# Moving the conversion of the first two weight tiles two pairs of heads ahead, in a fused attention and feed-forward kernel

## Chip, cores and metric

The kernel runs on one core of a Trainium2 chip. The metric is the device time of one execution in microseconds (us), as the median of several runs. TensorE is called PE here, VectorE DVE, ScalarE ACT, GpSimd POOL, and SP is the engine that issues the DMAs of this kernel. Each engine works through its own list of instructions in the order in which they stand.

## What is computed

Decay attention over 4 batches of 8 heads (576 positions, head size 64), then two feed-forward blocks on the 2304 x 512 result:

```python
scores = scale * np.matmul(q, k.transpose(0, 1, 3, 2))
decay = cum[:, :, :, None] - cum[:, :, None, :]        # cum: running sum of log f
scores = np.where(causal, -1e9, scores + decay)
attn = softmax(scores)                                  # max, exp, sum, divide
x = (attn @ v), heads side by side                      # 2304 x 512
h = np.maximum(x @ w_in, 0.0)                           # 512 -> 2048
x = h * h @ w_out                                       # 2048 -> 512
out = (sigmoid(x @ w_gate) * (x @ w_val)) @ w_out2      # 512 -> 1536 -> 512
```

Everything is wanted to float32 accuracy. The five weight matrices come in as float64.

## The kernel before

**Attention** works on 16 pairs of heads, p = 0 to 15. A pair goes through named steps, each a few instructions on one engine. S01, S2, S3 and S4 are the score matmuls on PE (L306, L379). R0a to R4 take the row minimum of the negated scores from PSUM on DVE (L284). X0a to X4 take the exponential on ACT (L292). N0, N2 and N3 form reciprocals of the row sums on DVE (L388, L389). M0a to M4 multiply by them on POOL (L394). G1 to G4 transpose on PE (L405, L411). E1 to E4 copy the transposed blocks into one SBUF tile, `pts`: E1 and E3 on ACT (L316), E2 and E4 on DVE (L318). PV multiplies by v on PE (L439, 14 matmuls in two passes each, so 28 in the trace: 8 that need E1 and E2, then 20 that need all of `pts`). xhi on ACT (L456) and xlo on DVE (L454) write the result into `xT`. All PSUM tiles of attention come from a ring of four, `pa0` to `pa3`, so a matmul can also wait for the step that read the tile's old contents.

The table ORDER (L471) is the pipeline. One iteration `it` runs every step of the table once, each for the pair `it - lag`, with the lag written behind the step. So in one iteration E3 and PV work on pair it - 2, while X4, X3, G and M work on it - 1 and S, R and X0 to X2 on `it`. The code of attention is under a manual schedule: its instructions stand on each engine as they are written. What comes after L497 is placed by a scheduler, which may put it among the last steps of attention too.

**Weights.** `w_load` (L103) loads one 512 KB tile of float64 words into a raw buffer, of which there are three. `w_conv` (L119) turns it into two float32 tiles, `hl`: an ACT step (L131), four DVE steps (L132, L133, L134, L137), an ACT step (L140) and a POOL step (L141), each waiting for the one before. L140 is issued on ACT right behind L131 when nothing is written between. `conv_load(n)` loads the first n tiles of the queue, `conv_some(1)` converts the next one. The first up-projection needs "in" tile 0 at its start and tile 1 some 12 us later.

The lines that place the first two tiles:

```python
if it == NP - 4:
    conv_load(2)
if it in (NP, NP + 1):
    conv_some(1)
```

NP is 16. Iterations 16 and 17 are the two in which no new pair starts: the pipeline drains there. A third tile, "out" tile 0, has a free raw buffer from the start and is loaded by the scheduler right behind the two.

**Feed-forward.** `up` (L516) does an up-projection block (L524) into a ring of eight PSUM banks, `down` (L565) a down-projection (L588). Between them the activations go to DRAM and back.

Of the kernel before, what the change touches and what calls it, by code (L numbers as in the profile page):

```python
# [40 lines left out]
def kernel(  # L41
# [17 lines left out]
    NP = BH // 2  # L59
# [85 lines left out]
    def conv_load(n):  # L145
        for key, m, _, _ in conv_q[:n]:
            if (key, m) not in wraw:
                w_load(key, m)

    def conv_some(n):  # L150
        for _ in range(min(n, len(conv_q))):
            w_conv(*conv_q.pop(0))
            conv_load(3)
# [334 lines left out]
    for it in range(min(lags), NP + max(lags)):  # L488
        for nm_, lag in steps:
            p = it - lag  # L490
            if 0 <= p < NP:
                STEP[nm_](p)
        if it == NP - 4:
            conv_load(2)
        if it in (NP, NP + 1):
            conv_some(1)
    order.__exit__(None, None, None)  # L497
    att.close()
# [152 lines left out]
```

## Time and profile before

| | us |
|---|---|
| median of 3 runs | 1052.91 (1052.67 to 1055.0) |
| the profiled execution | 1052.9 |
| its span, first to last instruction | 1051.2 |
| PE busy in the span | 1027.0 (98%) |
| attention, from the start to the first up-projection matmul | 209.3 |

The page's first part gives the busy time of each engine. The chain that ended last is followed back from the last instruction, at each step to what released it. The timeline gives each instruction with its start, its length, and in brackets the idle time of its engine in front of it with the engine, tile and line that ended it. The windows view cuts the span into stretches and gives for each the busy times and PEclk, the clock granted to PE (1.00 is 2.4 GHz, 0.50 is 1.2 GHz).

### The profile page before, as it was taken

What the parts mean: (1) busy time and instruction counts of PE and PEld (TensorE: products, weight loads), DVE (VectorE), ACT (ScalarE), POOL (GpSimd) and SP (SyncE); (2) the same over time, 40 slices, a digit from 0 to 9 for tenths busy, and PEclk for the clock granted to TensorE, in tenths of its full rate; (3) what the DMA queues carried; (4) which work ended last, traced back from release to release, by engine and by line L of the source; (5) the groups of instructions that cost most, each with busy time, mean ns of one, the idle gap of its engine ahead of it and who ended that gap; (6) DMA issues with size and microseconds to landing.
All of it is one profiled execution on the core that took longest, in us unless ns stands there. A gap on an engine that the chain in (4) does not pass through costs nothing.

```text
span 1051.2 us, 15632 instructions
## 1 busy us (share of the span) xinstructions
PE 1027.0 (98%) x5675; PEld 859.7 (82%) x5675; DVE 503.3 (48%) x1067; ACT 399.5 (38%) x854; POOL 220.7 (21%) x306
## 2 busy tenths in 40 slices
PE   4999999899999999999999999999999999999998
PEld 3788788588888888888888988888888888888887
DVE  2878778597666675233232414444444421232222
ACT  2888778544444343233232323222222211122222
POOL 3776666532122211000000002111111120000000
PEclk7999999899999999999999999999999999999999
DMA  5333333066765565333332214434433211244333
GB/s 121 71 86 87 70 83 106 21 187 199 210 211 188 188 204 167 101 93 98 101 93 83 85 51 119 132 124 132 132 119 107 94 46 46 78 138 140 99 123 110
DMA packets 125965, 121.98 MB, mean 116 GB/s; under 512 B 63552, under 2 KB 91200, under 8 KB 125888
## 3 DMA queue, kind: packets, MB, share of 16 engines
q1 hardware_dynamic: 125888, 120.99, 38.6%
q8 instruction: 44, 0.72, 0.3%
q14 instruction: 33, 0.27, 0.1%
HBM read 83.06 MB, written 37.90 MB: 115 GB/s over the span
## 4 chain that ended last, share of the span: by engine, by line
PE 95%; SPq 2%; DMA 1%; DVE 0%; issue 0%; ACT 0%; POOL 0%; POOLq 0%
PE ps L524 47%; PE ps L588 33%; PE pa L439 4%; PE pa L306 4%; PE pa L405 3%; PE pa L270 2%; PE pa L379 2%; SPq L196 1%; DMA cr<-cum_d 1%; PE pa L411 1%; SPq L200 1%; POOL pt L394 0%; ACT pt L292 0%; SPq L356 0%; ACT pts L316 0%
## 5 line engine op out<-in xcount | busy, mean ns | idle before, releaser
L524 PE MATMUL ps<-xT,hl 128*128 128x512 f32 (+1 forms) x2400 | 494.4, 368 | 0.0
L524 PEld LDWEIGHTS ps<-xT,hl 128*128 128x128 f32 x2400 | 418.4, 189 | 75.8
L141 POOL TENSOR_TENSOR hl<-wf,hl 128x512 fp32r<-128x512 f32 x68 | 93.1, 1377 | 565.1 <-ACT hl L140 548.6
L562 DVE TENSOR_TENSOR gg<-gi,gg 128x512 fp32r<-128x512 f32 (+1 forms) x140 | 90.5, 647 | 237.0 <-ACT gg L561 236.9
L588 PE MATMUL ps<-gg,hl 128*128 128x512 f32 (+1 forms) x960 | 197.3, 368 | 0.0
L588 PEld LDWEIGHTS ps<-gg,hl 128*128 128x128 f32 x960 | 167.2, 189 | 30.0
L561 ACT ACTIVATE gg<-gi 128x512 fp32r<-128x512 f32 (+1 forms) x140 | 82.4, 589 | 251.1 <-PE ps L588 227.8
L588 PE MATMUL ps<-hl,gg 128*128 128x512 f32 x648 | 147.1, 389 | 0.0
L588 PEld LDWEIGHTS ps<-hl,gg 128*128 128x128 f32 x648 | 121.6, 188 | 25.2
L394 POOL TENSOR_TENSOR pt<-pt,sm 128x128 f32<-128x128 f32 (+2 forms) x144 | 105.8, 767 | 53.8 <-DVE sm L389 53.8
L616 DVE TENSOR_TENSOR r<-ps,r 128x512 f32<-128x512 f32 (+1 forms) x60 | 38.2, 636 | 138.1 <-PE ps L524 133.3
L292 ACT ACTIVATE pt<-pt,nm 128x128 f32<-128x128 f32 (+1 forms) x144 | 82.5, 583 | 10.1 <-DVE nm L284 10.0
L137 DVE SCALAR_TENSOR_TENSOR wf<-wraw,wtmp 128x512 int32<-128x512 int32 x68 | 57.6, 848 | 57.4 <-POOL hl L141 56.0
L614 ACT ACTIVATE r<-ps 128x512 f32<-128x512 f32 (+1 forms) x60 | 32.9, 548 | 122.5 <-PE ps L524 122.5
L140 ACT ACTIVATE hl<-wf 128x512 fp32r<-128x512 f32 x68 | 42.9, 631 | 88.6 <-DVE wf L137 47.2
L131 ACT ACTIVATE wtmp<-wraw 128x512 f32<-128x512 f32 x68 | 45.2, 666 | 74.5 <-DMA wraw<-in_moe_w_in_dram 23.4
L284 DVE CUSTOM_DVE_ANT_0 pt<-pa,maskc 128x128 f32<-128x128 f32 (+2 forms) x144 | 67.0, 514 | 12.0 <-PE pa L306 11.4
L543 ACT ACTIVATE r<-ps 128x512 f32<-128x512 f32 (+1 forms) x80 | 42.5, 547 | 43.2 <-DMA g<-r 38.2
L544 DVE TENSOR_TENSOR r<-r 128x512 f32<-128x512 f32 (+1 forms) x80 | 50.7, 646 | 17.0 <-ACT r L543 17.0
L439 PE MATMUL pa<-pts,vn 128*64 128x320 f32 (+4 forms) x448 | 49.2, 371 | 3.9 <-ACT pts L316 3.9
L439 PEld LDWEIGHTS pa<-pts,vn 128*64 128x64 f32 x448 | 30.5, 141 | 22.9 <-ACT pts L316 4.4
L134 DVE SCALAR_TENSOR_TENSOR wtmp<-wraw,wtmp 128x512 int32<-128x512 int32 x68 | 48.0, 708 | 2.2
(79 smaller groups left out, 685.4 us busy)
## 6 DMA issues: line engine op xcount, KB each, us to landing
g<-r SPq DMA_DIRECT2D x112, 256.0 KB
gi<-g SPq DMA_DIRECT2D x112, 256.0 KB
wraw<-in_moe_w_out_dram SPq DMA_DIRECT2D x28, 512.0 KB
wraw<-in_moe_w_in_dram SPq DMA_DIRECT2D x16, 512.0 KB
wraw<-in_moe_w_gate_dram SPq DMA_DIRECT2D x12, 512.0 KB
wraw<-in_moe_w_val_dram SPq DMA_DIRECT2D x12, 512.0 KB
out_dram<-r SPq DMA_DIRECT2D x18, 256.0 KB
qn<-in_q_dram SPq DMA_DIRECT2D x32, 128.0 KB
```

What stands on the lines that cost most here:

```text
L134: nc.vector.scalar_tensor_tensor(out=xi, in0=hi, scalar=-0x40000000, in1=xi, op0=ALU.bitwise_and, op1=ALU.bitwise_or)
L137: nc.vector.scalar_tensor_tensor(out=t.bitcast(I32), in0=lo, scalar=29, in1=xi, op0=ALU.logical_shift_right, op1=ALU.bitwise_or)
L141: nc.gpsimd.tensor_tensor(out=hl[:, 1, :], in0=t, in1=hl.bitcast(F32)[:, 0, :], op=ALU.subtract)
L284: nc.vector.tensor_tensor_reduce(out=o, in0=s, in1=mask, scale=1.0, scalar=3.0e38, op0=ALU.add, op1=ALU.min, accum_out=nm_t[p % 2][:, c:c ...
L292: nc.scalar.activation(out=x, in_=x, func=AF.Exp, bias=nm_t[p % 2][:, c:c + 1], scale=-1.0, accum_out=sm_t[p % 2][:, c:c + 1])
L394: nc.gpsimd.tensor_tensor(out=x, in0=x, in1=sm_t[p % 2][:, c:c + 1].to_broadcast([128, e - a]), op=ALU.mult)
L439: nc.tensor.matmul(o[64 * h:64 * h + 64, 512 * half + s - lo:512 * half + hi - lo], lhsT=vn[:, c, h, :], rhs=pts[:, h * PW + c * PS + s:h ...
L524: nc.tensor.matmul(h[:, 0:n], lhsT=a, rhs=x[:, b_, :], start=(c == 0 and i == 0), stop=(c == KD - 1 and i == 2))
L544: nc.vector.tensor_tensor(out=r, in0=r, in1=r, op=ALU.mult)
L561: nc.scalar.activation(out=gg[:, 0, 0:n], in_=t, func=AF.Copy)
L562: nc.vector.tensor_tensor(out=gg[:, 1, 0:n], in0=t, in1=gg.bitcast(F32)[:, 0, 0:n], op=ALU.subtract)
L588: nc.tensor.matmul(o, lhsT=lhsT, rhs=rhs, start=(k_ == 0 and x == 0), stop=(last and x == 2))
```

## The change

The first two tiles are loaded after iteration 10 and not after iteration 12, and converted after iterations 14 and 15 and not after 16 and 17.

```diff
@@ -490,9 +490,9 @@
             p = it - lag
             if 0 <= p < NP:
                 STEP[nm_](p)
-        if it == NP - 4:
+        if it == NP - 6:
             conv_load(2)
-        if it in (NP, NP + 1):
+        if it in (NP - 2, NP - 1):
             conv_some(1)
     order.__exit__(None, None, None)
     att.close()
```

What this does to the lists of the engines. PE's list is the same. On ACT, at the border of iterations 14 and 15 (the L292 on `pt_245` are X of pair 14: a 128x128 and two 128x384 steps are X1 and X2, the 128x576 step is X4; L316 is E3 of pair 13):

```order
 L292 ACTIVATE pt_245,sm_248<-pt_245,nm_250 128x128
 L292 ACTIVATE pt_245,sm_248<-pt_245,nm_250 128x384 x2
+L131 ACTIVATE wtmp<-wraw 128x512
+L140 ACTIVATE hl<-wf 128x512
 L292 ACTIVATE pt_245,sm_248<-pt_245,nm_250 128x576
 L316 ACTIVATE pts<-pa_218 128x2x4x128
```

The two ACT steps of tile 0 stand between X2 and X4 of pair 14; E3 of pair 13 comes behind them. DVE has the four steps of this conversion directly behind R3 of pair 14, and POOL has L141 between M1a and M2a of pair 14.

On ACT, at the border of iterations 15 and 16 and in the drain (`pt_246` is pair 15; the first L316 is E3 of pair 14, the last one the first half of E1 of pair 15; L456 is xhi of pair 14):

```order
 L292 ACTIVATE pt_246,sm_249<-pt_246,nm_251 128x384 x2
+L131 ACTIVATE wtmp<-wraw 128x512 x2
+L140 ACTIVATE hl<-wf 128x512
 L292 ACTIVATE pt_246,sm_249<-pt_246,nm_251 128x576
 L316 ACTIVATE pts<-pa_219 128x2x4x128
 L292 ACTIVATE pt_246,sm_249<-pt_246,nm_251 128x512 x2
+L131 ACTIVATE wtmp<-wraw 128x512 x2
 L456 ACTIVATE xT_203<-pa_218 128x256
 L456 ACTIVATE xT_203<-pa_218 128x320
+L131 ACTIVATE wtmp<-wraw 128x512
 L316 ACTIVATE pts<-pa_219 128x2x256
```

Tile 1 and the first step of "out" tile 0 stand ahead of X4 of pair 15 and E3 of pair 14; first steps of three more tiles stand ahead of E1 and E3 of pair 15, where no L140 is left.

On DVE, the same border (L284 are the two R3 of pair 15, each with the read of its minimum; L389 is the reciprocal of N2):

```order
+L132 TENSOR_SCALAR wtmp<-wtmp 128x512
 L389 RECIPROCAL sm_249<-sm_249 128x2
+L133 TENSOR_SCALAR wtmp<-wtmp 128x512
+L134 SCALAR_TENSOR_TENSOR wtmp<-wraw,wtmp 128x512
 L284 ISA pt_246,nm_251<-pa_217,maskc 128x512
 L284 ISA nm_251 128x1
 L284 ISA pt_246,nm_251<-pa_217,maskc 128x512
 L284 ISA nm_251 128x1
+L132 TENSOR_SCALAR wtmp<-wtmp 128x512
+L133 TENSOR_SCALAR wtmp<-wtmp 128x512
+L134 SCALAR_TENSOR_TENSOR wtmp<-wraw,wtmp 128x512
+L137 SCALAR_TENSOR_TENSOR wf<-wraw,wtmp 128x512 x2
```

Three steps of "out" tile 0 stand ahead of R3 of pair 15, the four steps of tile 1 behind it. After N3 of pair 15 come seven steps of later tiles, ahead of xlo of pair 14, where none stood before. On SP the three loads move from behind the `cr` loads of iteration 12 to behind those of iteration 10.

## Rows read from the trace of the kernel before

**Rows 1.** The page, first part: span, then PE's busy time, share of the span and number of matmuls.

```profile
span 1051.2 us, 15632 instructions
PE 1027.0 (98%) x5675; PEld 859.7 (82%) x5675; DVE 503.3 (48%) x1067; ACT 399.5 (38%) x854; POOL 220.7 (21%) x306
```

**Rows 2.** The windows view: the stretch, its length, the busy time (and number) of PE, PEld, DVE, ACT and POOL, then PEclk, the DMA share and GB/s.

```profile
185.00:194.00 9.00, 9.00 (x83) 7.09 (x79) 7.09 (x27) 7.34 (x23) 6.34 (x10) 1.00 0.00 1
...
203.00:204.00 1.00, 0.00 (x0) 0.00 (x0) 0.36 (x1) 0.60 (x2) 0.00 (x0) 0.74 0.00 0
...
209.00:210.00 1.00, 1.00 (x8) 0.79 (x5) 0.00 (x0) 0.64 (x3) 0.00 (x0) 0.50 0.00 0
210.00:211.00 1.00, 1.00 (x6) 0.77 (x5) 0.90 (x3) 1.00 (x3) 0.00 (x0) 0.85 0.00 0
...
209.24:407.00 197.76, 197.76 (x960) 167.35 (x959) 140.87 (x234) 84.28 (x156) 45.10 (x34) 1.00 0.62 197
```

**Rows 3.** The chain that ended last, in the drain of attention: start, length, what.

```profile
200.29 0.82 DVE pts L318
...
203.93 1.01 ACT pts L316
...
204.99 4.32 PE pa L439 x20
209.31 2.74 PE ps L524 x9
```

**Rows 4.** The timeline of the drain, engine by engine: ACT, DVE, PE.

```profile
203.40 0.63 ACT L140 ACTIVATE hl<-wf 128x512 fp32r<-128x512 f32 x1 [4.62 <-DVE wf L137]
...
209.95 1.23 ACT L131 ACTIVATE wtmp<-wraw 128x512 f32<-128x512 f32 x2
...
197.23 0.82 DVE L454 TENSOR_TENSOR xT<-pa,xT 128x256 fp32r<-128x256 f32 x2 [1.11 <-ACT xT L456]
...
201.03 0.42 DVE L132 TENSOR_SCALAR wtmp<-wtmp 128x512 f32<-128x512 f32 x1
...
202.67 0.69 DVE L137 SCALAR_TENSOR_TENSOR wf<-wraw,wtmp 128x512 int32<-128x512 int32 x1
...
196.37 1.53 PE L405 MATMUL pa<-ident,pt 128*128 128x128 f32 x12
198.38 1.09 PE L405 MATMUL pa<-ident,pt 128*128 128x128 f32 x8 [0.49 <-POOL pt L394]
199.49 0.77 PE L411 MATMUL pa<-ident,pt 128*128 128x128 f32 x5
200.18 0.87 PE L439 MATMUL pa<-pts,vn 128*64 128x256 f32 x8
```

**Rows 5.** The timeline at the border of iterations 14 and 15: X4 of pair 14 and E3 of pair 13 on ACT, the first R0 of pair 15 on DVE (it follows R3 of pair 14 at once), PV of pair 13 on PE.

```profile
182.29 0.78 ACT L292 ACTIVATE pt<-pt,nm 128x576 f32<-128x576 f32 x1
...
183.05 1.02 ACT L316 ACTIVATE pts<-pa 128x1024 f32<-128x1024 f32 x1
...
185.25 0.29 DVE L284 CUSTOM_DVE_ANT_0 pt<-pa,maskc 128x128 f32<-128x128 f32 x1
...
184.50 2.92 PE L439 MATMUL pa<-pts,vn 128*64 128x256 f32 x28
```

**Rows 6.** The timeline at the border of iterations 15 and 16: X4 of pair 15, E3 of pair 14 and the second X3 of pair 15 on ACT, the two R3 of pair 15 on DVE, PV of pair 14 on PE.

```profile
192.34 0.77 ACT L292 ACTIVATE pt<-pt,nm 128x576 f32<-128x576 f32 x1
...
193.10 1.00 ACT L316 ACTIVATE pts<-pa 128x1024 f32<-128x1024 f32 x1
...
194.90 0.71 ACT L292 ACTIVATE pt<-pt,nm 128x512 f32<-128x512 f32 x1
...
193.45 0.69 DVE L284 CUSTOM_DVE_ANT_0 pt<-pa,maskc 128x512 f32<-128x512 f32 x1
...
194.06 0.69 DVE L284 CUSTOM_DVE_ANT_0 pt<-pa,maskc 128x512 f32<-128x512 f32 x1
...
193.34 3.10 PE L439 MATMUL pa<-pts,vn 128*64 128x256 f32 x28
```

**Rows 7.** DVE beside POOL: the timeline of M3 and M4 of pair 15 on POOL, of one L141 on POOL and an L133 that ran beside the next one on DVE; then the view of line L133, with the shortest, median and longest duration in ns.

```profile
196.29 3.14 POOL L394 TENSOR_TENSOR pt<-pt,sm 128x512 f32<-128x512 f32 x3 [0.41 <-DVE sm L389]
...
214.87 3.05 POOL L141 TENSOR_TENSOR hl<-wf,hl 128x512 fp32r<-128x512 f32 x2 [9.50 <-ACT hl L140]
...
216.80 1.40 DVE L133 TENSOR_SCALAR wtmp<-wtmp 128x512 int32<-128x512 int32 x1
...
L133 DVE TENSOR_SCALAR wtmp<-wtmp x68: 412/427/1401, 201.5 to 835.8; 128x512 int32<-128x512 int32 x68
```

**Rows 8.** Loads: the timeline of the DMA issues of SP (`cr` of iteration 10, `cr` and weight loads of iteration 12, a later weight load), the first matmul on that `cr` on PE, and the L131 on ACT that waited for the later weight load.

```profile
137.21 0.75 SPq L356 DMA_DIRECT2D cr<-cum_d  x2
...
159.85 0.75 SPq L356 DMA_DIRECT2D cr<-cum_d  x2
160.65 0.94 SPq L111 DMA_DIRECT2D wraw<-in_moe_w_in_dram  x2
...
214.19 0.40 SPq L111 DMA_DIRECT2D wraw<-in_moe_w_in_dram  x1
...
161.79 0.29 PE L306 MATMUL pa<-cr,one_l 64*128 64x128 f32 x2
...
219.14 0.68 ACT L131 ACTIVATE wtmp<-wraw 128x512 f32<-128x512 f32 x1 [2.71 <-DMA wraw<-in_moe_w_in_dram]
```

## Prediction

> **What bounds the kernel now.** I read the page's busy times first, then the chain that ended last, then the timeline of the last pairs of attention, where the edit lands. TensorE (PE) is busy 1027.0 of 1051.2 us [rows 1], so time is won or lost only where PE waits or runs at its lower clock. The feed-forward stages give nothing: in the first up-projection PE is busy 197.76 of 197.76 us [rows 2]. In the last pairs it is busy 9.00 of 9.00 us [rows 2]. The one wait near the edit is in the drain. The chain goes DVE's copy E4 at 200.29, ACT's copy E3 at 203.93, PE's last PV at 204.99, first up-projection matmul at 209.31 [rows 3]. Why E3 is late stands in the timeline: the input of E3 is there at 199.49, when PE goes on to the next transposes, but ACT sits 4.62 us in front of L140, the third step of a weight conversion, waiting for DVE's L137, and E3 stands behind it. PE is through with the first 8 matmuls of PV at 201.05 and idles 3.94 us [rows 3, 4]. In that idle time the granted clock falls (0.74 in the slice from 203 us), it is 0.50, the 1.2 GHz level, up to 210 and back at 2.4 GHz about 210.3, 5.3 us after matmuls resumed [rows 2].
>
> **What the change removes.** No conversion of a first-layer tile stands in front of E3 of pair 15 any more. Alone this would be worth: PV's last 20 matmuls start when E4 ends, at 201.17 and not at 204.99 (3.8); they take 2.92 - 0.87 = 2.0 us at the full clock [rows 4, 5] and not 4.32 [rows 3] (2.3); the up-projection starts at the full clock, where 1.05 us at half were worth 0.5. Sum 6.6 us.
>
> **What it adds: the same wait twice, earlier.** The order on ACT shows that L131 and L140 of tile 0 now stand between X2 and X4 of pair 14, ahead of E3 of pair 13, and those of tile 1, with an L131 of "out" tile 0, ahead of X4 of pair 15 and E3 of pair 14. L140 needs DVE's four steps, and the order on DVE puts these behind R3 of the same pair. I walk both places with the clock times of the trace of before.
>
> First place. DVE ends R3 of pair 14 at 185.25, where R0 of pair 15 starts today [rows 5]; now L132 starts there. From L132 to the end of L137 takes 2.33 us (201.03 to 203.36), L140 follows 0.04 later and what stands behind it 0.53 after that [rows 3, 4]. So X4 starts at 188.15 and not at 182.29: 5.86 us late. E3 starts 0.76 after it as before, at 188.91, ends at 189.91, and PV of pair 13 can start at 189.97. It could start at 184.50 before [rows 5] and writes the PSUM tile that E3 reads, so all 28 matmuls wait: **+5.5 us**. PE idles longer than in the drain of before, so I take it that the clock falls as there and comes back 5.3 us after the restart: half of 5.3 is lost, **+2.6 us**. Everything of the next round comes 8.1 us late, since PE has no slack there [rows 2].
>
> Second place, on the clock of before (8.1 to be added). Two L131 stand where X4 was, at 192.34, and take 1.23 us [rows 4, 6]: 193.57. DVE has L132 of "out" tile 0 there, the reciprocal, L133 and L134, together some 1.7 us, then the two R3 0.61 apart [rows 6], then the four steps of tile 1: 193.60 + 1.7 + 1.2 + 2.33 = 198.8. L140 at 198.86, X4 at 199.4, E3 at 200.2 to 201.2. PV of pair 14 runs its first 8 matmuls at 193.34 as today and then waits from 194.2 to 201.2: 7.0 us. Its other 20 run at half clock, 4.3 us as in the drain of before: it ends at 205.5 and not at 196.4 [rows 6], **+9.1 us**.
>
> Drain. From 205.5: 1.5 us of transposes (0.5 more while the clock is low, to 206.5), 1.1 and 0.8 us for the other two groups, E4 0.8 [rows 3, 4], PV's last part 2.0, with starts between: up-projection at 212.3, so 6.8 us after PV of pair 14. Before it was 209.3 - 196.4 = 12.9. This is where the removed wait and the clock go in: **-6.1 us**, and **-0.5 us** for the start of the up-projection.
>
> New in the drain are seven DVE steps of the second-layer and later tiles ahead of xlo of pair 14 (two rounds of 2.33 less one L137: 3.9 us). They start when the reciprocal N3 is through, 0.4 after X3 of pair 15 at 202.8, so about 203.3, end at 207.2, and xlo (0.8) [rows 4] is done at 208.0, before the transposes that need its PSUM tile (208.6). They cost nothing so far. But POOL works M3 and M4 at that time, 3.14 us [rows 7], and no row shows these steps beside an M step. The nearest row is L133 beside POOL's L141: 1.40 us in place of 0.43, ending 0.3 after the POOL steps [rows 7]. If each step waits for the POOL step it meets, only about four get through before M4 ends, xlo ends near 210.5 and the drain is 2.3 us longer. Bounds 0 and 2.3; I take the middle, **+1.2 us**, since a step that falls between two M steps waits for neither.
>
> The Trainium skill (SBUF — State Buffer, "Who interferes with whom") says that DVE and GpSimd hold a shared port pair as an exclusive lock for a whole instruction, so one blocks fully. By that rule the term would be its upper end, and the time 1.1 us more than below. The row of L133 agrees with it for L141; no row shows it for M.
>
> Loads. The three 512 KB loads go out behind the `cr` loads of round 10 (issued at 137.21) and not behind those of round 12. At the old place they went out at 160.65, right behind `cr` at 159.85, and the matmul on that `cr` ran at 161.79 without a wait [rows 8]. I take 0; 0.5 us is the most, a wait like the 0.3 us ones that PE has on `cr` elsewhere. Taking them from the old place gains nothing, PE had no wait there.
>
> **Sum.** 5.5 + 2.6 + 9.1 - 6.1 - 0.5 + 1.2 = 11.8 us later. The profiled execution took 1052.9 us (span 1051.2 and 1.7 around it), the median is 1052.91. Forecast **1064.7 us**.
>
> **Rivals.**
> *The conversion fits into idle time (faster).* From 185 to 194 us ACT is busy 7.34 and DVE 7.09 of 9.00 us [rows 2]: 1.66 and 1.91 free, against 1.3 us (L131, L140) and 2.2 us (four DVE steps). If E3 kept its time the change would give the 6.6 us of the drain: 1046.3. It decides at the point where E3 of pair 13 leaves ACT before 184.4. Against it: free time is a mean, E3 stands behind an instruction that waits on DVE, and the drain of before shows what follows [rows 4]. The Trainium skill (Perfetto Trace Analysis, "Optimization Strategy") says that interleaving regimes with different contended engines may improve performance, with occupancy as the measure for ACT and DVE; by that rule this rival is the outcome. Chance 0.04.
>
> *The clock holds.* If it stays at 2.4 GHz through both waits, 2.6 and 4.3 - 2.0 = 2.3 us fall away: 1059.8. For it: its fall took some 2.5 us of idle time and may come later. Against it: both new waits (5.5 and 7.0 us) are longer than the one in which it fell (3.94). Chance 0.13.
>
> *Late weight loads in the drain.* ACT has the L131 of two tiles whose loads wait for the raw buffers that the second conversion frees (about 199 us) ahead of E1 and E3 of pair 15. A load takes 5.0 us from issue to its L131 (214.19 to 219.14) [rows 8]: 204.5, in time. If the second runs behind the first it is there at 209.5, E3 starts near 210 and not at 208.6, and some 1.8 us are added: 1066.5. Chance 0.12.
>
> *Half of it.* One of the two waits is covered by something I do not see: 1054 to 1059.5. Chance 0.06. *The gains and losses cancel* within 0.2%, about what a measurement of this kernel can tell from no change: 0.02.
>
> **How the numbers follow.** 0.63 for the forecast, 0.04, 0.13, 0.12, 0.06 and 0.02 for the others. Only the first rival is faster: 0.04; same 0.02; slower 0.94. The range goes from 1059.5 (the clock holds) to 1067.5 (both ends of the POOL term and the late loads, 11.8 + 1.1 + 1.8): it leaves out the faster case, the half case and some of the spread, under 2 in 10.
>
> **What would show it.** In the trace after: an idle of PE of about 5.5 us before PV of pair 13 and one of about 7 us inside PV of pair 14, both released by E3 (L316), with ACT idle in front of L140 and DVE's L137 as releaser; the granted clock at 0.50 after each; no wait of PE for E3 in the last pair, and the first up-projection matmul near 221.6 us (209.3 + 11.8, and 0.5 that it gives back after that). The forecast is wrong if PV of pair 13 starts near 184.5; the sizes are wrong if the clock stays at 1.00, or if xlo of pair 14 comes long after PV.

## The result and the profile after

The changed kernel takes **1066.59 us** (median of 4 runs, 1065.01 to 1068.83); the kernel before, run beside it, 1053.39 (4 runs, 1052.67 to 1055.0). The ratio is 1.0125, with a 95% interval of 1.0100 to 1.0149: it is slower by 1.25%. The forecast was 1064.7 within 1059.5 to 1067.5.

The profiled execution of the changed kernel took 1068.83 us, the longest of its four. The page begins (compare [rows 1]):

```profile
span 1066.9 us, 15623 instructions
...
PE 1031.6 (97%) x5675; PEld 862.1 (81%) x5675; DVE 503.2 (47%) x1067; ACT 399.2 (37%) x854; POOL 220.3 (21%) x306
```

The work is the same, 5675 matmuls; PE is busy 4.6 us longer for it (part of it at the lower clock), and the span is 15.7 us longer. The view of waits of PE, what for, us in total, times, longest:

```profile
PE pa L439 <- ACT pts L316: 12.3, 2, 6.9
...
PE pa L411 <- DVE xT L454: 2.3, 1, 2.3
```

Before, PE waited for E3 (L316) once, 3.9 us, in the drain [rows 3, 4]. Now it does so twice, 12.3 us in all, and not in the drain. A new wait, for xlo (L454), has come in there.

**First border** (iterations 14 and 15; [rows 5] before). Timeline of ACT and DVE:

```profile
183.39 0.66 ACT L131 ACTIVATE wtmp<-wraw 128x512 f32<-128x512 f32 x1
...
186.35 0.42 DVE L132 TENSOR_SCALAR wtmp<-wtmp 128x512 f32<-128x512 f32 x1
...
187.99 0.69 DVE L137 SCALAR_TENSOR_TENSOR wf<-wraw,wtmp 128x512 int32<-128x512 int32 x1
...
188.72 0.63 ACT L140 ACTIVATE hl<-wf 128x512 fp32r<-128x512 f32 x1 [4.66 <-DVE wf L137]
...
189.25 0.76 ACT L292 ACTIVATE pt<-pt,nm 128x576 f32<-128x576 f32 x1
...
190.01 1.00 ACT L316 ACTIVATE pts<-pa 128x1024 f32<-128x1024 f32 x1
```

ACT is through with L131 at 184.05 and stands still for 4.66 us in front of L140, a step of 0.63 us. X4 (189.25) and E3 (190.01) need nothing of the weight tile. They are late only because they stand behind it in ACT's order. PE pays for it (chain of waits: start, length, what; the length covers PV of pair 13 alone):

```profile
191.07 5.60 PE pa L439 x28
```

That PV had been free to start at 185.67 (its wait is 5.40 us) and takes 5.60 where it took 2.92 [rows 5]. Windows view, columns as in [rows 2], the granted clock is the third number from the end:

```profile
190.00:197.00 7.00, 5.93 (x30) 3.49 (x32) 0.57 (x2) 2.71 (x9) 5.96 (x7) 0.51 0.19 70
197.00:198.00 1.00, 1.00 (x11) 0.75 (x10) 0.54 (x2) 1.00 (x5) 0.00 (x0) 0.99 0.00 0
...
208.00:214.00 6.00, 3.52 (x14) 1.71 (x16) 2.77 (x7) 4.82 (x10) 4.75 (x6) 0.50 0.49 175
...
220.00:222.00 2.00, 1.60 (x12) 0.92 (x12) 1.97 (x4) 0.11 (x1) 0.00 (x0) 0.73 0.39 136
222.00:224.00 2.00, 2.00 (x10) 0.98 (x8) 0.03 (x1) 0.00 (x0) 0.00 (x0) 0.50 0.00 0
```

The clock is at 1.2 GHz from the end of the wait until 197.0, 5.9 us after the restart. From the first border to the up-projection there are three such stretches, where the kernel before has one.

**Second border** (iterations 15 and 16; [rows 6]), timeline of ACT, DVE and then PE:

```profile
201.48 1.21 ACT L131 ACTIVATE wtmp<-wraw 128x512 f32<-128x512 f32 x2
...
208.14 0.63 ACT L140 ACTIVATE hl<-wf 128x512 fp32r<-128x512 f32 x1 [5.44 <-DVE wf L137]
...
209.43 1.00 ACT L316 ACTIVATE pts<-pa 128x1024 f32<-128x1024 f32 x1
...
207.41 1.29 DVE L137 SCALAR_TENSOR_TENSOR wf<-wraw,wtmp 128x512 int32<-128x512 int32 x2
...
202.76 0.87 PE L439 MATMUL pa<-pts,vn 128*64 128x256 f32 x8
...
210.49 4.04 PE L439 MATMUL pa<-pts,vn 128*64 128x320 f32 x20 [6.86 <-ACT pts L316]
```

The same pattern, 6.86 us of idle inside PV of pair 14 and then 20 matmuls at the lower clock.

**Drain** ([rows 4, 7]), timeline of POOL, DVE and PE:

```profile
212.66 3.56 POOL L394 TENSOR_TENSOR pt<-pt,sm 128x512 f32<-128x512 f32 x3 [0.41 <-DVE sm L389]
...
212.89 1.14 DVE L133 TENSOR_SCALAR wtmp<-wtmp 128x512 int32<-128x512 int32 x1
213.96 1.26 DVE L132 TENSOR_SCALAR wtmp<-wtmp 128x512 f32<-128x512 f32 x1
...
215.14 1.63 DVE L134 SCALAR_TENSOR_TENSOR wtmp<-wraw,wtmp 128x512 int32<-128x512 int32 x1
...
218.23 0.81 DVE L454 TENSOR_TENSOR xT<-pa,xT 128x256 fp32r<-128x256 f32 x2
...
214.45 2.40 PE L405 MATMUL pa<-ident,pt 128*128 128x128 f32 x20
...
219.19 0.74 PE L411 MATMUL pa<-ident,pt 128*128 128x128 f32 x5 [2.33 <-DVE xT L454]
...
221.12 3.84 PE L439 MATMUL pa<-pts,vn 128*64 128x320 f32 x20 [0.40 <-DVE pts L318]
...
224.89 1.43 PE L524 MATMUL ps<-xT,hl 128*128 128x512 f32 x5
```

Conversion steps of later tiles stand ahead of xlo of pair 14. Beside POOL's multiplies (212.66 to 216.22) they take 1.14, 1.26 and 1.63 us where they take 0.43, 0.42 and 0.69 alone. PE waits 2.33 us for xlo. The clock falls a third time about 1.7 us after that wait (0.73 in the slice from 220 us), and the last part of PV takes 3.84 us.

Behind that nothing has moved but the start of the first phase. The chain of the kernel before, and that of the changed one, each with its first up-projection and the phase behind it:

```profile
209.31 198.11 PE ps L524 x960
407.42 197.16 PE ps L588 x960
```

```profile
224.96 197.64 PE ps L524 x960
422.60 197.16 PE ps L588 x960
```

So all but 1.2 us of the difference in span lies between the moment at which PE could start PV of pair 13 and the first up-projection matmul. I measure every kernel by these two marks, with the start of PV of pair 14 between them. Before: 184.50, 193.34, 209.24, so 8.84 and 15.90 us. After: 185.67, 202.76, 224.89, so 17.09 and 22.13, together **14.5 us more**. (The 0.47 us by which the first phase is shorter are lost again behind the last matmul.) The other 1.2 us of the difference in span were there before the edit's place was reached: PE waits now and then for a `cr` load in the first 140 us, and not at the same places in each execution. The medians differ by 13.2.

### The profile page after: what moved, and what is told of

Read it like the earlier page. It is cut to its first block, busy times and chain, and to the rows that moved or that the text cites. A ratio compares the mean times of both kernels' runs of the same rounds, so it can differ in the third digit from the quotient of the medians.

```text
span 1066.9 us, 15623 instructions
## 1 busy us (share of the span) xinstructions
PE 1031.6 (97%) x5675; PEld 862.1 (81%) x5675; DVE 503.2 (47%) x1067; ACT 399.2 (37%) x854; POOL 220.3 (21%) x306
## 4 chain that ended last, share of the span: by engine, by line
PE 93%; DVE 2%; SPq 2%; ACT 1%; DMA 1%; issue 1%; DVEq 0%; ACTq 0%
PE ps L524 46%; PE ps L588 32%; PE pa L439 4%; PE pa L306 4%; PE pa L405 3%; PE pa L270 2%; PE pa L379 1%; SPq L196 1%; DMA cr<-cum_d 1%; SPq L200 1%; PE pa L411 1%; ACT pt L292 1%; DVE wtmp L134 0%; DVE wtmp L132 0%; DVE pts L318 0%
## 5 line engine op out<-in xcount | busy, mean ns | idle before, releaser
L141 POOL TENSOR_TENSOR hl<-wf,hl 128x512 fp32r<-128x512 f32 x68 | 92.4, 1365 | 576.4 <-ACT hl L140 576.2
L137 DVE SCALAR_TENSOR_TENSOR wf<-wraw,wtmp 128x512 int32<-128x512 int32 x68 | 58.6, 864 | 60.7 <-POOL hl L141 59.6
L292 ACT ACTIVATE pt<-pt,nm 128x128 f32<-128x128 f32 (+1 forms) x144 | 82.5, 583 | 9.4 <-DVE nm L284 9.4
L140 ACT ACTIVATE hl<-wf 128x512 fp32r<-128x512 f32 x68 | 42.8, 631 | 93.0 <-DVE wf L137 51.6
L284 DVE CUSTOM_DVE_ANT_0 pt<-pa,maskc 128x128 f32<-128x128 f32 (+2 forms) x144 | 67.1, 514 | 12.4 <-PE pa L306 11.6
L131 ACT ACTIVATE wtmp<-wraw 128x512 f32<-128x512 f32 x68 | 45.1, 666 | 68.1 <-DMA wraw<-in_moe_w_in_dram 17.1
L439 PE MATMUL pa<-pts,vn 128*64 128x320 f32 (+4 forms) x448 | 53.3, 392 | 12.7 <-ACT pts L316 12.3
```

Of the source, the lines that this page charges most:

```text
L137: nc.vector.scalar_tensor_tensor(out=t.bitcast(I32), in0=lo, scalar=29, in1=xi, op0=ALU.logical_shift_right, op1=ALU.bitwise_or)
L141: nc.gpsimd.tensor_tensor(out=hl[:, 1, :], in0=t, in1=hl.bitcast(F32)[:, 0, :], op=ALU.subtract)
L284: nc.vector.tensor_tensor_reduce(out=o, in0=s, in1=mask, scale=1.0, scalar=3.0e38, op0=ALU.add, op1=ALU.min, accum_out=nm_t[p % 2][:, c:c ...
L292: nc.scalar.activation(out=x, in_=x, func=AF.Exp, bias=nm_t[p % 2][:, c:c + 1], scale=-1.0, accum_out=sm_t[p % 2][:, c:c + 1])
L439: nc.tensor.matmul(o[64 * h:64 * h + 64, 512 * half + s - lo:512 * half + hi - lo], lhsT=vn[:, c, h, :], rhs=pts[:, h * PW + c * PS + s:h ...
```

## The experiments

Ten kernels. An edit shifts the line numbers behind it by a few; the names of the tiles stay. "Against before" is the difference of medians to the kernel before on the same chip. The last two columns are the stretches between the marks, as the profile of each has them, less those of the kernel before (8.84 and 15.90).

| kernel | median, us | against before | ratio, 95% interval | PV 13 to PV 14 | PV 14 to up-projection |
|---|---|---|---|---|---|
| changed | 1066.59 | +13.2 | 1.0100 to 1.0149 | +8.25 | +6.2 |
| e1_loads_only | 1053.84 | +0.2 | 0.9989 to 1.0008 | 0 | 0 |
| e3_first_only | 1055.46 | +1.8 | 1.0010 to 1.0029 | +7.6 | -5.8 |
| e4_second_only | 1054.33 | +0.6 | 0.9997 to 1.0016 | 0 | +1.2 |
| e2_first_split | 1050.05 | -3.9 | 0.9948 to 0.9978 | +1.6 | -5.5 |
| e6_drain_split | 1049.65 | -4.3 | 0.9945 to 0.9974 | 0 | -5.2 |
| e7_later_tiles_late | 1063.95 | +10.0 | 1.0072 to 1.0105 | +8.05 | +0.9 |
| e5_busy | 1065.18 | +11.5 | 1.0095 to 1.0128 | +10.0 for both | |
| e9_both_split | 1055.16 | +1.8 | 1.0010 to 1.0030 | +1.6 | -0.1 |
| e8_spread | 1054.04 | +0.7 | 0.9996 to 1.0015 | +3.1 | -5.8 |
| e10_slots | 1047.82 | -6.6 | 0.9928 to 0.9955 | 0 | -5.8 |

Theory: ACT works strictly in its order, so a short step that waits for DVE (hl, L140) holds the exponentials and E3 behind it, PE runs dry, and the clock falls on top. Rivals: the earlier loads cost time; the conversion is simply too much work for DVE at that place; the clock costs nothing.

**e1_loads_only.** The loads alone:

```diff
-        if it == NP - 4:
+        if it == NP - 6:
             conv_load(2)
```

> The kernel before with the loads of the two weight tiles issued two pairs sooner and nothing else moved. My theory: the loads cost nothing, so the time is that of the kernel before, 1053.4 us within 1. Rival, earlier loads push SP's other work: a time above 1055 and waits of PE on DMA landings near pair 11 that the kernel before doesn't have.

Both stretches are those of the kernel before to 0.01 us. The loads are out.

**e3_first_only and e4_second_only.** One tile moved each, loads as in the changed kernel. First e3, then e4:

```diff
-        if it in (NP - 2, NP - 1):
+        if it in (NP - 2, NP + 1):
             conv_some(1)
```

```diff
-        if it in (NP - 2, NP - 1):
+        if it == NP - 1:
+            conv_some(1)
+        if it == NP + 1:
             conv_some(1)
```

> Loads two pairs sooner; tile 0 converted after pair 14's iteration as in the changed kernel, tile 1 left where the kernel before has it, behind the last iteration. My theory: the wait of ACT's last conversion step for DVE's comes back (PE waits about 5.4 us for pts of pair 13), the clock's time at half after it costs 3.0 more, and the drain, with nothing of tile 0 in it, loses 6.6 of its wait against the kernel before, since no conversion step is left in front of its exponentials: 1053.4 + 5.4 + 3.0 - 6.6 = 1055.2. Rival, the drain's waits come from the conversion of any tile: tile 1's steps keep 3 or more of the 6.6, and the time is 1058 or more. Rival, the wait at pair 14's border comes only when both tiles move: 1047.

> Loads two pairs sooner; tile 0 converted in the last iteration but one of the two that the changed kernel uses (the border of pairs 14 and 15), tile 1 behind the last iteration as before. My theory: a wait of PE of 5.2 us for pts of pair 14 (that of the first border, moved), 2.1 for the cold matmuls behind it, the drain 6.1 shorter, the up-projection 0.5 shorter: 1053.4 + 5.2 + 2.1 - 6.1 - 0.5 = 1054.1. Rival, the drain of the changed kernel is long because of the border just ahead of it, not because of what is pulled into the drain: the drain stays at 10 us or more from the end of PV of pair 14 and the time is 1057 or more.

Both came out at the number that the theory gave (1055.2 and 1054.1), and none of the rivals did. PE's wait for E3 in the timeline of e3 and then of e4:

```profile
190.81 5.12 PE L439 MATMUL pa<-pts,vn 128*64 128x256 f32 x28 [5.39 <-ACT pts L316]
```

```profile
199.61 4.32 PE L439 MATMUL pa<-pts,vn 128*64 128x320 f32 x20 [5.18 <-ACT pts L316]
```

A tile that is moved up takes a wait of 5.2 to 5.4 us with it, at either border, and shortens the drain: with the lower clock, e3 pays 7.6 us at its border and gets 5.8 back. A third effect shows in the sum: +1.8 and +0.6 make 2.4, the two together cost 13.2. Moving one tile frees the drain already (there is one such wait there, for tile 0), so the second tile pays for a wait and wins nothing. With both gone from the end, conversions of later tiles move up into the last border and the drain, ahead of X4, E3 and xlo; in e3 and e4 none stands there, and e7 below takes them away.

**e2_first_split.** e3 once more, with two of tile 0's seven conversion steps elsewhere: `conv_end` has hl on ACT and lo on POOL (hl is L145 and PV L444 here):

```diff
+            if nm_ == "M4" and held:
+                conv_end(*held.pop())
...
+        if it == NP - 2:
+            held.append(w_conv(*conv_q.pop(0), late=True))
+        if it == NP + 1:
+            conv_some(1)
```

> As e3_first_only, but tile 0's last two steps (ACT's hl and POOL's lo, which wait for DVE's wf) stand behind the M4 step of the next iteration and not ahead of E3. All work of e3_first_only is there, at the same border; only the place of the two steps in the engines' order differs. My theory (ACT's exponentials are held behind a short step that waits for DVE): no PE wait at the border of pairs 13 and 14, the clock stays up, and with the drain 6.6 shorter the time is 1053.4 - 6.6 + about 1 for X and R steps that come later = 1047 to 1048.5. Rival, the DVE work itself doesn't fit at that border: PE still waits 3 us or more for pts, and the time is that of e3_first_only, 1055.

This decides between the theory and the amount of work. All DVE steps of e3 are there, at the same place, and PE's wait for E3 is gone:

```profile
186.13 2.92 PE L444 MATMUL pa<-pts,vn 128*64 128x256 f32 x28
...
186.70 0.86 DVE L132 TENSOR_SCALAR wtmp<-wtmp 128x512 f32<-128x512 f32 x1
...
187.60 0.93 DVE L133 TENSOR_SCALAR wtmp<-wtmp 128x512 int32<-128x512 int32 x1
...
193.71 0.62 ACT L145 ACTIVATE hl<-wf 128x512 fp32r<-128x512 f32 x1
...
196.58 2.92 PE L444 MATMUL pa<-pts,vn 128*64 128x256 f32 x28
```

PV of pair 13 starts without a wait, the clock stays up, and the kernel is 5.7 us faster against its own before than e3 (-3.9 against +1.8). It missed its range (1047 to 1048.5) by 1.6 us: the border is 10.45 us long, not 8.84. DVE's steps do cost something there. L132 and L133 ran beside POOL's multiplies and took 0.86 and 0.93 us. The run moves hl and lo together; that hl on ACT is the one that counts is read from PE's wait, which ends with ACT's E3 in e3 and in the changed kernel.

**e6_drain_split.** The same edit in the drain of the kernel before, whose wait it should remove: hl and lo of tile 0 behind E3 of the second drain iteration.

```diff
+            if nm_ == "E3" and held:
+                conv_end(*held.pop())
...
+        if it == NP:
+            held.append(w_conv(*conv_q.pop(0), late=True))
+        if it == NP + 1:
+            conv_some(1)
```

> The kernel before, its loads and its borders untouched, with tile 0's hl and lo moved behind the E3 step of the drain's second iteration. My theory: the 4.6 us for which ACT's exponentials of pair 15 stood behind hl go from the drain, and the cold matmuls behind that wait run at the full clock in part: 1053.4 - 4.6 = 1048.8, between 1048.0 and 1049.5. Rival, the drain is bound by DVE's sums and xT anyway: within 1 of 1053.4.

-4.3 us, where -4.6 was expected; the time, 1049.65, is 0.15 us above its range, and the kernel before beside it took 1053.91 and not the 1053.4 from which the range was worked out. ACT's E3 is now at 201.11 and hl at 204.93, in the order that the data allow. PE's next waits are for hl and lo, at the first up-projection matmuls on tile 0. The table's second mark is the first of these lines; all but two of the matmuls run from the second line on, 1.4 us later:

```profile
205.61 0.73 PE L534 MATMUL ps<-xT,hl 128*128 128x512 f32 x2 [0.54 <-ACT hl L145]
206.98 7.33 PE L534 MATMUL ps<-xT,hl 128*128 128x512 f32 x31 [0.63 <-POOL hl L146]
```

**e7_later_tiles_late.** The changed kernel without the steps of later tiles in the last border and the drain; their loads are tied to the end of attention by an ACT copy of one element into each raw tile.

```diff
+        if after_x[0]:
+            nc.scalar.activation(out=raw[:, 0:1], in_=xT[3].bitcast(F32)[:, 1, NT - 1:NT], func=AF.Copy)
...
+    after_x[0] = True
     conv_load(3)
+    after_x[0] = False
```

> The changed kernel, both tiles converted where it has them, but the first three weight tiles behind these are held back (an ACT copy of one element ties their raw tiles to the end of attention), so that no step of theirs stands in the last border or in the drain. My theory: PE's second wait falls from 6.9 to 5.2 us, the stretch from the end of PV of pair 14 to the first up-projection matmul from 10.45 to about 6.8 us, and the up-projection's first phase may lose up to 0.5 to its later loads: 1066.6 - 1.7 - 3.6 = 1061.3, up to 1063. Rival, the late drain comes from the border ahead of it: that stretch stays at 9.5 or more, and the time is 1064.5 or more.

By the marks the gain is what the theory gave: the stretch from PV of pair 14 on is 16.83 us against 22.13, 5.3 less. The second wait is 5.19 us, not 6.86. The drain, timeline of PE:

```profile
210.14 4.32 PE L442 MATMUL pa<-pts,vn 128*64 128x320 f32 x20 [5.19 <-ACT pts L319]
...
218.70 2.27 PE L442 MATMUL pa<-pts,vn 128*64 128x320 f32 x20 [0.21 <-DVE pts L321]
220.91 5.30 PE L527 MATMUL ps<-xT,hl 128*128 128x512 f32 x22
```

From the end of PV of pair 14 (214.46) to the up-projection it takes 6.5 us, where the changed kernel takes 10.4, and the last PV part runs at the full clock (2.27, not 3.84). The rival wanted 9.5 us or more there, and it did not come. The median, 1063.95, missed the expected 1061.3 to 1063: less of the 5.3 us shows in the times, 2.6 us between the two medians and 3.2 when each is taken against its own kernel before. The profiled execution reached the first mark 1.5 us later than that of the changed kernel. Ahead of that mark the two differ only in one load, which the changed kernel issues at 140.11 and e7 behind attention. Whether such lateness makes up all of the rest stays open.

**e5_busy.** The changed kernel with 28 spare matmuls ahead of PV of pairs 13 and 14, to keep PE at work during the waits:

```diff
+        if p in (NP - 3, NP - 2):
+            d = qk[p % 2]
+            for _ in range(28):
+                nc.tensor.matmul(
+                    spare[p][:, 0:512], lhsT=one_l[:, 0:128], rhs=d["kh"][:, 0:512], start=True, stop=True
+                )
```

> The changed kernel with 28 spare matmuls of 128x512, results unused, ahead of PV of pair 13 and as many ahead of PV of pair 14: about 5.8 us of work at full clock, put where PE waits 5.4 and 6.9 us. Nothing of the computation is left out. My theory: the waits stay as stretches in which nothing useful runs, but the granted clock does not fall to 0.50 behind them, so the 3.0 us lost at half clock behind the first wait come back, less 0.4 by which the spare work outlasts the wait; behind the second, 2.1 of cold matmuls come back unless the drain's chain over DVE takes them again. 1066.6 - 2.7 = 1063.9, down to 1061.9. Rival, the clock is not what makes the stretches behind the waits long: 1066.6 or more, up to 1068.4 with the spare work on top.

The part of the clock in the mechanism is borne out: in the windows view the clock is 1.00 through both borders and the drain. One line, then PV of pair 13 (L448 here) and the wait for xlo in the drain from the timeline:

```profile
191.00:197.00 6.00, 6.00 (x44) 4.21 (x44) 1.12 (x6) 3.27 (x9) 5.45 (x7) 1.00 0.30 89
```

```profile
193.90 2.93 PE L448 MATMUL pa<-pts,vn 128*64 128x256 f32 x28
...
217.66 0.74 PE L413 MATMUL pa<-ident,pt 128*128 128x128 f32 x5 [1.57 <-DVE xT L463]
```

PV takes 2.93 us, not 5.60. By the marks 4.5 us come back (34.75 against 39.22). By the medians it is 1.4: 1065.18 lies between the expected 1063.9 and the rival's 1066.6, and the two intervals against before overlap, so the times settle neither the size nor the rival. What speaks against the rival is the length of the stretches in the trace. Part of the gain was given away: the spare work took 6.66 us where the wait was 5.40.

**e9_both_split.** The changed kernel with hl and lo of both tiles behind the M4 step of the next iteration. The place where `held` is emptied is that of e2 and is left out here; `conv_load(3)` is what `conv_some` does too:

```diff
         if it in (NP - 2, NP - 1):
-            conv_some(1)
+            held.append(w_conv(*conv_q.pop(0), late=True))
+            conv_load(3)
```

> The changed kernel with one thing moved: the last two steps of each tile's conversion (ACT's hl and POOL's lo) stand behind the M4 step of the next iteration, not at the border. All four conversion steps ahead of them stay where the change put them. My theory: neither border has the wait of 5.4 and 6.9 us, the clock stays up, and each border keeps only the 1.6 us that e2_first_split's did; the drain still has steps of later tiles in it, some 8.5 us against 12.9 in the kernel before: 1053.7 + 1.6 + 1.8 - 4.4 = 1052.7, between 1050 and 1055. Rival, two tiles' DVE work in front of the last pairs is itself too much: PE waits 3 us or more at the second border and the time is 1058 or more.

1055.16: the place of these two short steps makes 11.4 of the 13.2 us. But it is above the 1052.7 expected and 0.16 us above the range, and the rival has a part: the drain is no shorter than before (15.79 against 15.90). PE waits in it for POOL's multiply of pair 15 (L399). Timeline of DVE and PE:

```profile
203.01 0.16 DVE L394 RECIPROCAL sm<-sm 128x3 f32<-128x3 f32 x1
...
205.43 1.97 PE L410 MATMUL pa<-ident,pt 128*128 128x128 f32 x8 [4.36 <-POOL pt L399]
```

The chain goes back from there to the reciprocal of pair 15 at 203.01, which DVE reaches only among the steps of two conversions (198.12 to 203.08), those of tile 1 and of "out" tile 0. Behind the wait the granted clock is 0.50 up to 210, so this drain has both prices. With twice the steps at one border, DVE is late for the multiplies too.

**e8_spread.** An attempt at a version that beats both: tile 0's conversion in four pieces, one behind the G2 step of each of iterations 12 to 15. `w_steps` is the conversion as a generator that gives one piece at each `next`:

```diff
+            if nm_ == "G2" and NP - 4 <= it < NP:
+                if it == NP - 4:
+                    held = w_steps(*conv_q.pop(0))
+                next(held, None)
```

> A version meant to beat both: the loads four pairs sooner, tile 0's conversion cut into four pieces of one or two steps, one piece behind the G2 step of each of the iterations 12 to 15, where POOL has no multiply under way; tile 1 behind the last iteration as before. My theory: DVE gives 0.9 us or less in any one iteration, so PE waits for nothing at the borders, and the drain is about 7 us where the kernel before has 12.9: 1053.7 - 5.9 + 0.5 to 1.5 for DVE's steps that come later = 1048.3 to 1049.3. Rival, DVE has no room even for that: every piece comes through in full, 2.3 us in sum, and the time is 1050 or more, as e2_first_split's.

A miss, 1054.04. The drain gave the 5.8 us, and two pieces took most of them back: 3.1 us between the marks, and 2.1 us in iteration 12, ahead of the first mark, so that the table does not have them. Together that is -0.6; what makes up the 1.3 us from there to the +0.7 of the medians stays open. Timeline of DVE and PE in iteration 12, then of POOL and PE in iteration 15:

```profile
162.38 0.43 DVE L136 TENSOR_SCALAR wtmp<-wtmp 128x512 f32<-128x512 f32 x1 [2.71 <-ACT wtmp L135]
...
164.07 0.74 PE L418 MATMUL pa<-ident,pt 128*128 128x128 f32 x5 [2.10 <-DVE kl L367]
...
196.42 1.27 POOL L148 TENSOR_TENSOR hl<-wf,hl 128x512 fp32r<-128x512 f32 x1 [3.11 <-ACT hl L147]
...
198.85 0.77 PE L418 MATMUL pa<-ident,pt 128*128 128x128 f32 x5 [2.87 <-POOL pt L401]
```

I had made the mistake that I was studying: L136 on DVE waits 2.71 us for ACT's Abs with kl behind it, and lo on POOL waits 3.11 us for hl with a multiply behind it. The amount of DVE work was not the cause: two steps of 0.43 us cost PE 2.10.

**e10_slots.** The same pieces, one step each, where the trace of the kernel before shows the engine idle, and each a whole phase behind the step whose result it reads.

```diff
+    PIECES = [(NP - 6, "X3a")] + [(NP - i, "N3") for i in (5, 4, 3, 2)] + [(NP - 1, "X3a"), (NP - 1, "M4")]
...
+            if (it, nm_) in PIECES:
+                next(held, None)
```

> As e8_spread, but each piece of tile 0's conversion put where its engine idles in the trace of the kernel before and where no other engine is behind it: the Abs step behind X3a of iteration 10 (ACT idles 1.2 us there, before xhi), one DVE step behind N3 of each of iterations 11 to 14 (DVE idles 1.4 us there, before xlo), hl behind X3a and POOL's lo behind M4 of iteration 15 (POOL idles 2.2 us there). Loads six pairs sooner, tile 1 as in the kernel before. My theory (what cost time in e8_spread was where the steps stood, kl behind a step that waited for ACT's Abs 2.1 us and the last multiply behind POOL's lo 2.9 us): no PE wait at any border, and the drain about 7 us against 12.9: 1053.4 - 5.9 = 1047.5, up to 1048.5. Rival, any DVE step inside attention pushes PE in full: 2.2 to 4 us come back and the time is 1049.7 or more.

1047.82, as expected, 6.6 us under the kernel before (ratio 0.9942) and the fastest of all. Its timeline shows DVE's four pieces at 0.40, 0.40, 0.66 and 0.66 us; the first two and lo:

```profile
143.73 0.40 DVE L137 TENSOR_SCALAR wtmp<-wtmp 128x512 f32<-128x512 f32 x1
...
154.96 0.40 DVE L139 TENSOR_SCALAR wtmp<-wtmp 128x512 int32<-128x512 int32 x1
...
191.46 1.28 POOL L151 TENSOR_TENSOR hl<-wf,hl 128x512 fp32r<-128x512 f32 x1
```

PE waits for none of them: from PV of pair 9 to that of pair 13 it is 44.15 us (43.95 before), and from there to PV of pair 14 8.84, as before.

## Why the prediction was right, step by step

The sign and the mechanism of the two waits were right, and the time lies within the range; one term was too small. That the range held was in part luck. Its upper end contains 1.8 us for late weight loads, which did not come. Without them it is 1052.9 + 11.8 + 1.1 = 1065.8, and the measured 1066.59 lies above that.

- **First wait, +5.5.** It measured 5.40, with the late X4 and E3 that the walk gave. e3 has it alone, and e2 takes it away by moving hl and lo: the cause is shown.
- **Clock after it, +2.6.** The lower clock held 5.9 us after the restart, not 5.3, so half of that, 3.0, was lost. The 5.3 was carried over from the one earlier case, and that it came so near is luck: behind the second wait the clock was back 3.6 us after the restart (0.95 in the slice from 214 us). The next PV came 8.25 us late (8.1 in the prediction). e5 shows that the clock stays up when PE has work in the wait. The rival that the clock holds did not come.
- **Second wait and cold PV, +9.1.** The wait measured 6.86 (7.0) and the 20 matmuls 4.04 (4.3); PV of pair 14 takes 11.77 us from start to end where it took 3.10, so +8.7. e7 and e4 show what the "out" tile's steps add: without them the wait is 5.2.
- **The drain, -6.1 + 1.2.** This is the mis-sized step, "I take the middle, +1.2 us". From the end of PV of pair 14 (214.53) to the first up-projection matmul it takes 10.4 us where the prediction had 6.8 + 1.2 = 8.0. The seven steps have a price of 3.6 us, and the bounds, 0 to 2.3, did not hold it. Two things made it up. xlo ended 4.5 us after PV of pair 14, nearer the prediction's upper end (5.0) than its middle, and PE's wait for it is 2.33 us. And the prediction did not follow the clock behind that wait: the last PV part took 3.84 and not the 2.27 us of e7. (The upper end itself does not follow from the prediction's times: 210.5 is 1.9 us after 208.6, not 2.3.) e7 shows that the steps of later tiles are the cause of all of it (6.5 us without them).
- **Why the later steps cost so much there.** That it is their place beside POOL's multiplies, and not their number, rests on the rows of 1.14, 1.26 and 1.63 us, which are 2.5 us over their usual lengths. xlo ended at 219.04; an estimate without these 2.5 us is 216.55, before PE comes to wait for it at 216.86. In e5 only four of the seven steps stand ahead of xlo, the same three are as long (1.15, 1.26 and 1.63 us), and PE still waits 1.57 us. No run took the steps away from POOL's multiplies and left their number.
- **The rule weighed there.** The last of the three long DVE steps ends 0.55 us after POOL's multiplies (216.77 and 216.22), and the three multiplies take 3.56 and not 3.14 us. The Trainium skill (SBUF — State Buffer, "Who interferes with whom") says that of DVE and GpSimd whoever takes the shared port pair first keeps it for the whole instruction, and the other fully blocks. By that rule the term would have been its upper end, 2.3 us; PE's wait for xlo, 2.33 us, is nearer to that than to the middle that I took.
- **Start of the up-projection, -0.5.** Its first phase takes 197.64 and not 198.11: -0.47.
- **Loads, 0.** e1: no difference in either stretch. The rival of late weight loads in the drain did not come: L131 there waited for a buffer that DVE's L137 gives back, not for a load.
- **The conversion fits into idle time (rival).** It did not, in the place chosen by the change. By the prediction's own figures DVE's 2.2 us were more than the 1.91 us that it had free there. The free time was there all the same: e10 converts tile 0 in attention without a wait of PE. What decided was the order at the border.

In the profiled execution the terms come to 8.25 + 8.7 - 2.4 (the drain, from 12.8 to 10.4) = 14.5 at the first up-projection matmul, and 14.0 behind the first phase, against 11.8 forecast and 13.2 by medians.

## What to carry to other kernels

An engine with free time is not a place for a step that waits for another engine: before a step is moved, read what stands behind it in that engine's order and when its input will be there. A chain over several engines that is cut into single steps, each put where its own engine idles and well after the step that feeds it, can cost nothing that shows, as in e10; the same steps in one block cost 7 to 9 us at each border here, the clock included. And a wait of PE has a second price in the stretch behind it, at the lower clock, so every wait that a prediction adds is followed up to the clock, the small ones too.

## What was not expected of the hardware

In the drain of the changed kernel the granted clock stood at 0.50 in the slice from 222 to 224 us, behind a wait of only 2.33 us and a pause of 0.40 soon after it. It was still 1.00 during that wait and fell about when the pause ended. The prediction had followed the clock only behind waits of 3.9 us and more. In e8_spread PE waited 2.87 us for a multiply and the clock did not fall; windows view of the stretch behind that wait:

```profile
200.00:202.00 2.00, 2.00 (x22) 1.19 (x20) 1.93 (x6) 0.47 (x1) 1.18 (x3) 1.00 0.03 8
```

What PE did before the two waits differs: in the drain of the changed kernel it had come back from the lower clock about 2.8 us before the wait (0.95 in the slice from 214 us, idle from 216.85), in e8 it had been busy at the full clock for the whole iteration. No run tried whether that is what decides.
